# Moving the w2 product of an MLP block into the attention loop that precedes it, and its residual and statistics to other engines

## The chip, the core and the metric

The kernel runs on one core of a Trainium2 chip. The metric is the device time of one execution in microseconds (us). The unchanged kernel took 329.89 us (median of 3 runs, 329.3 to 330.42). "PE" is TensorE, whose matmuls write PSUM; "DVE" is VectorE; "ACT" is ScalarE; "POOL" is GpSimd, which here mostly issues DMAs. Each engine has an instruction stream of its own; for each wait the profile names the instruction or DMA that ended it, which it infers from semaphores.

## The reference

One sequence of S = 2048 tokens, width D = 512, bfloat16:

```python
xn = layernorm(x)
s  = A(xn)            # 32 heads of 16; each token attends to 8 tokens, 2 apart; then @ wo
g  = silu(B(xn))
out = x + s * g

def B(x):             # x is xn here
    h  = gelu(layernorm(x) @ w1)
    # each quarter of h's columns is shifted by one or two tokens, forwards or backwards
    hs = concat(shift(h, -1), shift(h, +1), shift(h, -2), shift(h, +2)) @ w2
    x1 = x + hs
    return x1 + gelu(layernorm(x1) @ w3) @ w4      # w3: 512 x 1376
```

Tokens lie in 16 tiles of 128. Attention goes in 4 passes of 4 tiles. Attention and the product with w2 both need results of earlier stages, but neither needs the other.

## The kernel before

The attention loop of one pass, cut. DVE forms the products of q with shifted k (`prodT`), PE sums them per head (`lgA`, `lgB`), ACT takes `exp`, PE transposes, DVE normalises, DVE forms the products with shifted v (`prodpv`), PE adds the eight of a tile into `po`, ACT copies it out, PE transposes it to `oT`.

```python
attv = paw.enter_context(tc.tile_pool(name="attv", bufs=2))
psL  = paw.enter_context(tc.tile_pool(name="psL", bufs=2, space=bass.MemoryType.PSUM))
for ps_ in range(NPASS):
    lgA = psL.tile([P, 512], dt.float32, name="lgA", tag="lg")
    lgB = psL.tile([P, 512], dt.float32, name="lgB", tag="lg")
    # ... 8 x prodT on DVE, 32 matmuls into lgA / lgB; exp on ACT; expR on PE; softmax on DVE ...
    for tb in range(4):
        t = 4 * ps_ + tb
        po = psA.tile([P, 512], dt.float32, name="po", tag="pA")
        vsh = attv.tile([P, W, D], dt.bfloat16, name="vsh")
        nc.gpsimd.dma_start(out=vsh[:], in_=src)              # 1 MB, 8 shifted copies of v
        for hf in range(2):
            prodpv = att4.tile([P, 4, D], dt.bfloat16, name="prodpv")
            nc.vector.tensor_tensor(out=prodpv[:]..., in0=vsh[:, 4*hf:4*hf+4, :]..., in1=Pn[...], op=ALU.mult)
            for wv in range(4):
                nc.tensor.matmul(po[:], lhsT=ident[:], rhs=prodpv[:, wv, :], ...)
        # ... ost (ACT), otp (PE), oT (ACT) ...
```

After the whole of attention comes the stage that the change takes apart, called "hs" below:

```python
for t in range(NT):
    pt = psB.tile([P, 512], dt.float32, name="pt_hs", tag="pT")
    for i in range(CH):                                            # CH = 4
        st0 = MGH + t * P + shifts[i]
        nc.tensor.matmul(pt[:], lhsT=hT[:, i, st0:st0 + P], rhs=w2s[:, i, :], start=(i == 0), stop=(i == CH - 1))
    nc.vector.tensor_tensor(out=x1[:, t, :], in0=pt[:], in1=xn[:, t, :], op=ALU.add)
    nc.vector.bn_stats(out=stats2[:, t, :], in_=x1[:, t, :])
    nc.vector.bn_aggr(out=mv2[:, t, :], in_=stats2[:, t, :])
nc.scalar.activation(out=rstd2[:], in_=mv2[:, :, 1:2], func=ACT.Sqrt, bias=eps_t[:], scale=1.0)
nc.vector.reciprocal(out=rstd2[:], in_=rstd2[:])
# ... then 4 units of: x2b = (x1 - mean) * rstd, transpose, @ w3, gelu, @ w4, epilogue ...
```

One `rstd2` serves all 16 tiles, so the first `x2b` cannot start before the last tile's statistics are there. The first start of `x2b` is therefore a good mark for the end of everything before the w3 stage.

The softmax here doesn't subtract the row's maximum and nothing guards it: scores larger than these inputs give would overflow.

## Time and profile before

| | before |
|---|---|
| profiled span | 328.5 us |
| busy: PE / DVE / ACT | 241.2 / 238.5 / 148.2 us |
| attention on DVE: first prodT to end of last prodpv | 99.8 to 197.1 us |
| hs stage and its lead-in, to the first x2b | 197.1 to 224.0 us |
| w3, gelu, w4 and epilogue, to the end | 104.5 us |

The page of the kernel before: the busy times, then the span in 40 slices of 8.2 us, each digit the busy share in tenths; PEclk is the clock granted to PE in tenths of full speed.

```profile
PE 241.2 (73%) x1216; PEld 105.8 (32%) x1216; DVE 238.5 (73%) x469; ACT 148.2 (45%) x240; POOL 57.9 (18%) x97
...
PE   0004899999943577588476587777799999999992
...
DVE  0879200002999999989997963995979979969964
...
PEclk9999999999995559959989659999999999999998
```

Slices 12 to 23 are attention: DVE is at 9 and PE between 3 and 8, with a clock that falls to half speed and comes back. Slices 24 to 27 are the hs stage. The averages of 73% for both engines hide this: each is the limit in another stage.

The groups of instructions, by line and shape: count, then busy us and mean ns of one, then idle time of the engine just before them and what ended it.

```profile
L280 PE MATMUL po<-prodpv,ident 128*128 128x512 bf16 x128 | 42.6, 485 | 7.2 <-DVE prodpv L273 7.0
L273 DVE TENSOR_TENSOR prodpv<-vsh,Pn 128x2048 bf16<-128x2048 bf16 x32 | 38.1, 1203 | 5.5 <-DMA vsh<-vscr 5.5
...
L310 PE MATMUL pt_hs<-w2s,hT 128*128 128x512 bf16 x64 | 15.2, 378 | 4.7 <-DVE x L311 4.0 <-ACT oT L287 0.7
L311 DVE TENSOR_TENSOR x<-pt_hs,xn 128x512 bf16<-128x512 f32 x16 | 10.5, 658 | 5.7 <-PE pt_hs L310 5.7
L312 DVE BATCH_NORM_STATS2 stats<-x 128x6 f32<-128x512 bf16 x16 | 10.3, 679 | 0.0
...
L313 DVE BATCH_NORM_AGGREGATE mv<-stats 128x2 f32<-128x6 f32 x16 | 2.7, 166 | 0.0
```

L311 to L313 are 23.5 us of DVE work. While it runs, PE has 15.2 us of matmuls to do and waits on DVE for 4.0 us; ACT has almost nothing. The 5.5 us before L273 are stalls in attention for the 1 MB loads of `vsh`, of which two buffers exist.

The timeline at the end of attention and around the hs stage (start, duration, engine, line, operation, tiles, count; in brackets the idle time before and what ended it).

```profile
193.41 3.54 PE L280 MATMUL po<-prodpv,ident 128*128 128x512 bf16 x8
194.70 2.36 DVE L273 TENSOR_TENSOR prodpv<-vsh,Pn 128x2048 bf16<-128x2048 bf16 x2 [1.20 <-DMA vsh<-vscr]
...
197.93 1.89 PE L280 MATMUL po<-prodpv,ident 128*128 128x512 bf16 x8
...
202.77 0.69 DVE L311 TENSOR_TENSOR x<-pt_hs,xn 128x512 bf16<-128x512 f32 x1 [5.71 <-PE pt_hs L310]
...
223.68 0.25 DVE L315 RECIPROCAL rstd<-rstd 128x16 f32<-128x16 f32 x1 [0.37 <-ACT rstd L314]
223.97 0.74 DVE L324 TENSOR_SCALAR x2b<-x,mv,rstd 128x512 bf16<-128x512 bf16 x2
```

DVE ends attention at 194.70 + 2.36 = 197.06 us, waits 5.71 us for the last two tiles to pass through PE and ACT, and then works 21 us without a break worth naming. Note the two `po` lines: the same eight matmuls take 3.54 us at one time and 1.89 us at another. That is the clock.

The windows view of the same run: length, busy time and count of each engine, granted clock, DMA share, GB/s.

```profile
100.00:113.00 13.00, 6.55 (x44) 1.86 (x43) 12.67 (x20) 3.11 (x4) 1.80 (x2) 0.50 0.45 163
113.00:136.00 23.00, 15.82 (x93) 5.96 (x93) 22.22 (x30) 5.88 (x10) 3.53 (x4) 0.81 0.50 181
...
181.00:198.00 17.00, 11.93 (x39) 4.20 (x37) 13.29 (x20) 2.98 (x5) 2.15 (x3) 0.60 0.42 149
```

Read across, the engines are PE, PE's weight loads, DVE, ACT and POOL. In the second row DVE is busy 22.22 of 23 us, and PE 15.82 at a mean clock of 0.81. The same view for the hs stage, one row:

```profile
201.00:224.00 23.00, 17.12 (x72) 6.90 (x71) 20.75 (x50) 2.19 (x3) 1.09 (x2) 1.00 0.28 100
```

Here the clock is 1.00 and DVE is busy 20.75 us from 202.77 on: a faster PE could shorten the wait ahead of this stage, but not these 21 us.

### The profile page before, as it was taken

Reading aid. Unit: us, or ns where it says so; the run is one execution under the profiler, and the core shown is the slowest. Engines: PE = TensorE matmul, PEld = TensorE weight load, DVE = VectorE, ACT = ScalarE, POOL = GpSimd, SP = SyncE. Lnnn points to the kernel's source line nnn. Section 1 sums busy time; section 2 is a strip of 40 time slices with the busy share of each in tenths; the row PEclk is TensorE's granted clock in tenths of the full one; section 3 lists DMA queues with packets and bytes.
Section 4 is the critical chain, followed back from the end, with each engine's and each line's share of the span. In section 5 each row is a group of like instructions: output and inputs, shape, how many; then the busy total and the mean of one; then the engine's idle time right before and its main releaser. Section 6 shows DMA issues by size and latency. Waiting matters only on the chain.

```text
span 328.5 us, 3542 instructions
## 1 busy us (share of the span) xinstructions
PE 241.2 (73%) x1216; PEld 105.8 (32%) x1216; DVE 238.5 (73%) x469; ACT 148.2 (45%) x240; POOL 57.9 (18%) x97
## 2 busy tenths in 40 slices
PE   0004899999943577588476587777799999999992
PEld 0003544444310222132122223333344444444440
DVE  0879200002999999989997963995979979969964
ACT  0023866667974022213223024005898479477320
POOL 4770000054002011122022103000000311211231
PEclk9999999999995559959989659999999999999998
DMA  7645440023001526546357358200000110210221
GB/s 252 218 145 122 96 66 0 0 113 130 16 0 45 213 89 233 189 151 236 126 190 254 129 196 301 75 2 1 0 2 0 64 65 2 75 52 18 80 80 48
DMA packets 19904, 33.46 MB, mean 102 GB/s; under 512 B 10176, under 2 KB 12240, under 8 KB 19888
## 3 DMA queue, kind: packets, MB, share of 16 engines
q0 software_dynamic: 8016, 26.60, 22.9%
q1 hardware_dynamic: 9760, 4.56, 6.1%
q10 hardware_dynamic: 2112, 2.10, 1.9%
q8 instruction: 9, 0.15, 0.2%
q14 instruction: 7, 0.06, 0.1%
HBM read 26.94 MB, written 4.21 MB: 95 GB/s over the span
## 4 chain that ended last, share of the span: by engine, by line
PE 34%; DVE 29%; DMA 12%; issue 10%; ACT 10%; POOL 3%; POOLq 0%; DVEq 0%; ACTq 0%
DMA vsh<-vscr 9%; PE pt_qk L163 8%; PE pt_w L335 8%; PE pt_w L360 5%; PE pt_v L175 4%; PE po L280 4%; DVE prodpv L273 4%; DVE stats L312 3%; DVE x L311 3%; DMA wvtmp<-in_A_wqkv_dram 3%; DVE prodT L223 2%; ACT yT L157 2%; ACT ub L350 2%; DVE xn L148 2%; DVE bout L365 2%
## 5 line engine op out<-in xcount | busy, mean ns | idle before, releaser
L280 PE MATMUL po<-prodpv,ident 128*128 128x512 bf16 x128 | 42.6, 485 | 7.2 <-DVE prodpv L273 7.0
L360 PE MATMUL pt_w<-w4s,zb 128*128 128x512 bf16 (+1 forms) x176 | 42.4, 379 | 0.0
L273 DVE TENSOR_TENSOR prodpv<-vsh,Pn 128x2048 bf16<-128x2048 bf16 x32 | 38.1, 1203 | 5.5 <-DMA vsh<-vscr 5.5
L335 PE MATMUL pt_w<-x2Tp,w3s 128*128 128x512 bf16 (+1 forms) x176 | 39.9, 379 | 2.3 <-ACT zb L340 2.0
L195 DVE TENSOR_TENSOR ub<-zb 128x512 bf16<-128x512 bf16 x16 | 6.6, 418 | 43.9 <-ACT zb L192 43.8
L223 DVE TENSOR_TENSOR prodT<-qT,kT 128x2048 bf16<-128x2048 bf16 x32 | 37.8, 1211 | 0.1
L270 POOL DMA_DIRECT2D vsh<-vscr x16 | 14.2, 886 | 90.1 <-DVE prodpv L273 68.3
L282 ACT ACTIVATE ost<-po 128x512 bf16<-128x512 f32 x16 | 9.6, 597 | 44.8 <-PE po L280 44.8
L155 PE MATMUL ytp<-ident,ybt 128*128 128x128 bf16 x64 | 6.8, 259 | 30.1 <-DVE ybt L152 29.4
L340 ACT ACTIVATE zb<-pt_w 128x512 bf16<-128x512 f32 (+1 forms) x44 | 25.3, 594 | 7.2 <-PE pt_w L335 7.0
L163 PE MATMUL pt_qk<-xnT,wqk 128*128 128x512 bf16 x128 | 27.8, 379 | 0.1
L377 POOL DMA_DIRECT2D out_dram<-ob x16 | 8.9, 558 | 105.5 <-DVE ob L376 105.5
L350 ACT ACTIVATE ub<-ub 128x1536 bf16<-128x1536 bf16 (+2 forms) x20 | 22.9, 1145 | 7.2 <-DVE ub L349 7.0
L335 PEld LDWEIGHTS <-w3s 128*128 128x128 bf16 (+1 forms) x176 | 17.6, 100 | 23.3 <-issue 4.3
L280 PEld LDWEIGHTS <-ident 128*128 128x128 bf16 x128 | 14.6, 117 | 27.6 <-issue 21.8
L360 PEld LDWEIGHTS <-zb 128*128 128x128 bf16 (+1 forms) x176 | 16.9, 98 | 19.3 <-DVE zb L351 0.4
L228 PE MATMUL lgA<-prodT,E 128*32 128x512 bf16 x64 | 8.3, 506 | 16.5 <-DVE prodT L223 16.4
L347 DVE TENSOR_TENSOR ub<-zb 128x1536 bf16<-128x1536 bf16 (+2 forms) x20 | 14.7, 739 | 7.3 <-ACT zb L340 7.1
L310 PE MATMUL pt_hs<-w2s,hT 128*128 128x512 bf16 x64 | 15.2, 378 | 4.7 <-DVE x L311 4.0
L178 POOL DMA_DIRECT2D vscr<-vst x16 | 8.7, 542 | 54.3 <-ACT vst L177 54.1
L163 PEld LDWEIGHTS <-wqk 128*128 128x128 bf16 x128 | 12.5, 98 | 15.1 <-issue 0.2
L367 ACT ACTIVATE sgo<-bout 128x512 bf16<-128x512 bf16 x16 | 10.0, 627 | 15.7 <-DVE bout L365 15.6
(86 smaller groups left out, 392.0 us busy)
## 6 DMA issues: line engine op xcount, KB each, us to landing
vsh<-vscr POOLq DMA_DIRECT2D x16, 1024.0 KB, 5.7
x_sb<-in_A_x_dram ACTq DMA_DIRECT2D x4, 512.0 KB, 10.2
vscr<-vst POOLq DMA_DIRECT2D x16, 128.0 KB, 2.0
xr<-in_A_x_dram POOLq DMA_DIRECT2D x16, 128.0 KB, 2.4
out_dram<-ob POOLq DMA_DIRECT2D x16, 128.0 KB, 2.0
w3s<-in_B_w_dram SPq DMA_DIRECT2D x1, 1376.0 KB, 7.0
w4s<-in_B_w_dram POOLq DMA_DIRECT2D x1, 1280.0 KB, 9.4
wqk<-in_A_wqkv_dram SPq DMA_DIRECT2D x1, 1024.0 KB, 7.6
```

The lines of the kernel that those rows point to most:

```text
L163: nc.tensor.matmul(pt[:], lhsT=wqk[:, c, 128 * j:128 * j + 128], rhs=xnT[:, 4 * ps_:4 * ps_ + 4, c, :], start=(c == 0), stop=(c == CH - 1),)
L175: nc.tensor.matmul(pt[:], lhsT=xnT[:, t, c, :], rhs=wvp[:, c, :], start=(c == 0), stop=(c == CH - 1))
L223: nc.vector.tensor_tensor(out=prodT[:], in0=qT[:, c, 512 * ps_:512 * ps_ + 512].unsqueeze(1).broadcast_to([P, 4, 512]), in1=kwin, op=ALU.mult,
L270: nc.gpsimd.dma_start(out=vsh[:], in_=src)
L273: nc.vector.tensor_tensor(out=prodpv[:].rearrange("p w (dh h) -> p w dh h", dh=DH), in0=vsh[:, 4 * hf:4 * hf + 4, :].rearrange("p w (dh h) ...
L280: nc.tensor.matmul(po[:], lhsT=ident[:], rhs=prodpv[:, wv, :], start=(hf == 0 and wv == 0), stop=(hf == 1 and wv == 3))
L310: nc.tensor.matmul(pt[:], lhsT=hT[:, i, st0:st0 + P], rhs=w2s[:, i, :], start=(i == 0), stop=(i == CH - 1))
L335: nc.tensor.matmul(pt[0:kj, :], lhsT=w3s[:, c, 128 * jj:128 * jj + kj], rhs=x2Tp[:, :, c, :], start=(c == 0), stop=(c == CH - 1),)
L340: nc.scalar.activation(out=zb[0:kj, jj, :], in_=pt[0:kj, :], func=ACT.Copy)
L347: nc.vector.tensor_tensor(out=ub[0:kj, j0:j1, :], in0=zb[0:kj, j0:j1, :], in1=zb[0:kj, j0:j1, :], op=ALU.mult)
L350: nc.scalar.activation(out=ub[0:kj, j0:j1, :], in_=ub[0:kj, j0:j1, :], func=ACT.Sigmoid, scale=GELU_K1)
L360: nc.tensor.matmul(pt[:], lhsT=h2p[0:kj, jj, tb * P:(tb + 1) * P], rhs=w4s[0:kj, jj, :], start=(jj == 0), stop=(jj == FCH - 1),)
```

## The change

Its intent is to take the hs stage off the critical path. The w2 matmuls go into the attention loop, where PE has room. The three DVE operations of a tile go away: the residual `xn` is added by four more matmuls into the same PSUM bank (transposed `xn` against slices of an identity), and the statistics come as accumulated sums of two ACT passes over that bank, a copy and a square. It also doubles the `vsh` buffers and loads w3 earlier. The core of the diff (the four units of the last stage are also renamed, with no effect on what they do):

```diff
+    identX = const.tile([P, CH, D], dt.bfloat16, name="identX")
+    nc.vector.memset(identX[:], 0.0)
+    for c in range(CH):
+        nc.vector.tensor_copy(out=identX[:, c, c * P:(c + 1) * P], in_=ident[:])
...
+            w3s = wts.tile([P, CH, F], dt.bfloat16, name="w3s")
+            # one element, so that the load cannot be issued before the last yT is there
+            nc.vector.tensor_copy(out=w3s[0:1, 0, 0:1], in_=yT[0:1, NT - 1, 0, 0:1])
+            nc.sync.dma_start(out=w3s[:], in_=B_w3.rearrange("(c p) n -> p c n", p=P))
...
-            attv = paw.enter_context(tc.tile_pool(name="attv", bufs=2))
+            attv = paw.enter_context(tc.tile_pool(name="attv", bufs=4))
... at the end of each attention pass:
+                for tb in range(4):
+                    t = 4 * ps_ + tb
+                    pths = psL.tile([P, 512], dt.float32, name="pt_hs", tag="lg")
+                    for i in range(CH):
+                        st0 = MGH + t * P + [-1, +1, -2, +2][i]
+                        nc.tensor.matmul(pths[:], lhsT=hT[:, i, st0:st0 + P], rhs=w2s[:, i, :], start=(i == 0), stop=False)
+                    for c in range(CH):
+                        nc.tensor.matmul(pths[:], lhsT=xnT[:, t, c, :], rhs=identX[:, c, :], start=False, stop=(c == CH - 1))
+                    nc.scalar.activation(out=x1[:, t, :], in_=pths[:], func=ACT.Copy, accum_out=sum2[:, t:t + 1])
+                    nc.scalar.activation(out=junk[:], in_=pths[:], func=ACT.Square, accum_out=sumsq2[:, t:t + 1])
... after the last pass:
+            # mean2 = sum2/D; rstd2 = 1/sqrt(sumsq2/D - mean2^2 + eps): four small DVE ops, Sqrt on ACT, reciprocal on DVE
... and the hs stage after attention is removed:
-            for t in range(NT):
-                pt = psB.tile([P, 512], dt.float32, name="pt_hs", tag="pT")
-                ...
-                nc.vector.tensor_tensor(out=x1[:, t, :], in0=pt[:], in1=xn[:, t, :], op=ALU.add)
-                nc.vector.bn_stats(out=stats2[:, t, :], in_=x1[:, t, :])
-                nc.vector.bn_aggr(out=mv2[:, t, :], in_=stats2[:, t, :])
```

More of the change, by code (lines that the diff above doesn't have):

```diff
@@ L111 @@
         hT = pre.tile([P, CH, MGH + S + MGH], dt.bfloat16, name="hT")
+        xnT = pre.tile([P, NT, CH, P], dt.bfloat16, name="xnT")
+        x1 = xn
+        sum2 = pre.tile([P, NT], dt.float32, name="sum2")
+        sumsq2 = pre.tile([P, NT], dt.float32, name="sumsq2")
+        mean2 = pre.tile([P, NT], dt.float32, name="mean2")
+        rstd2 = pre.tile([P, NT], dt.float32, name="rstd2")
+        junk = pre.tile([P, D], dt.bfloat16, name="junk", bufs=1)
         nc.vector.memset(hT[:, :, 0:MGH], 0.0)
@@ L122 @@
             xtp = tc.alloc_tile_pool(name="xtp", bufs=1)
-            xnT = xtp.tile([P, NT, CH, P], dt.bfloat16, name="xnT")
             yT = xtp.tile([P, NT, CH, P], dt.bfloat16, name="yT")
@@ L287 @@
                     nc.scalar.activation(out=oT[:, t, :, :], in_=otp[:], func=ACT.Copy)
+                for tb in range(4):
[8 more added lines that the diff above has]
+                    nc.scalar.activation(out=junk[:], in_=pths[:], func=ACT.Square, accum_out=sumsq2[:, t:t + 1])
+            shifts = [-1, +1, -2, +2]
+            nc.vector.tensor_scalar(out=mean2[:], in0=sum2[:], scalar1=1.0 / D, scalar2=None, op0=ALU.mult)
+            msq = pre.tile([P, NT], dt.float32, name="msq")
+            nc.vector.tensor_tensor(out=msq[:], in0=mean2[:], in1=mean2[:], op=ALU.mult)
+            nc.vector.tensor_scalar(out=rstd2[:], in0=sumsq2[:], scalar1=1.0 / D, scalar2=None, op0=ALU.mult)
+            nc.vector.tensor_tensor(out=rstd2[:], in0=rstd2[:], in1=msq[:], op=ALU.subtract)
+            nc.scalar.activation(out=rstd2[:], in_=rstd2[:], func=ACT.Sqrt, bias=eps_t[:], scale=1.0)
+            nc.vector.reciprocal(out=rstd2[:], in_=rstd2[:])
         with ExitStack() as phB:
@@ L293 @@
             psB = phB.enter_context(tc.tile_pool(name="psB", bufs=2, space=bass.MemoryType.PSUM))
-            w3s = b2k.tile([P, CH, F], dt.bfloat16, name="w3s")
-            nc.sync.dma_start(out=w3s[:], in_=B_w3.rearrange("(c p) n -> p c n", p=P))
             w4s = b2k.tile([P, FCH, D], dt.bfloat16, name="w4s")
@@ L299, with stage_x2_w3 @@
             nc.gpsimd.dma_start(out=w4s[0:FLAST, FCH - 1, :], in_=B_w4[(FCH - 1) * P:F, :])
-            shifts = [-1, +1, -2, +2]
-            x1 = b2k.tile([P, NT, D], dt.bfloat16, name="x1")
-            stats2 = b2k.tile([P, NT, 6], dt.float32, name="stats2")
-            mv2 = b2k.tile([P, NT, 2], dt.float32, name="mv2")
-            rstd2 = b2k.tile([P, NT, 1], dt.float32, name="rstd2")
-            for t in range(NT):
-                pt = psB.tile([P, 512], dt.float32, name="pt_hs", tag="pT")
-                for i in range(CH):
-                    st0 = MGH + t * P + shifts[i]
-                    nc.tensor.matmul(pt[:], lhsT=hT[:, i, st0:st0 + P], rhs=w2s[:, i, :], start=(i == 0), stop=(i == CH - 1))
-                nc.vector.tensor_tensor(out=x1[:, t, :], in0=pt[:], in1=xn[:, t, :], op=ALU.add)
-                nc.vector.bn_stats(out=stats2[:, t, :], in_=x1[:, t, :])
-                nc.vector.bn_aggr(out=mv2[:, t, :], in_=stats2[:, t, :])
-            nc.scalar.activation(out=rstd2[:], in_=mv2[:, :, 1:2], func=ACT.Sqrt, bias=eps_t[:], scale=1.0)
-            nc.vector.reciprocal(out=rstd2[:], in_=rstd2[:])
-            zbs = {}
-            def stage_x2_w3(ps_):
-                x2Tp = b2w.tile([P, 4, CH, P], dt.bfloat16, name="x2Tp")
-                for tb in range(4):
-                    t = 4 * ps_ + tb
+            zbs = {}
+            units = [list(range(4 * i, 4 * i + 4)) for i in range(NPASS)]
+            def stage_x2_w3(uq):
+                tiles = units[uq]
+                QT = P * len(tiles)
+                x2Tq = b2w.tile([P, 4, CH, P], dt.bfloat16, name="x2Tq")
+                for tb, t in enumerate(tiles):
                     x2b = b2w.tile([P, D], dt.bfloat16, name="x2b")
-                    nc.vector.tensor_scalar(out=x2b[:], in0=x1[:, t, :], scalar1=mv2[:, t, 0:1], scalar2=rstd2[:, t, :], op0=ALU.subtract, op1=ALU.mult)
+                    nc.vector.tensor_scalar(out=x2b[:], in0=x1[:, t, :], scalar1=mean2[:, t:t + 1], scalar2=rstd2[:, t:t + 1], op0=ALU.subtract, op1=ALU.mult)
                     x2ps = psB.tile([P, CH, P], dt.bfloat16, name="x2ps", tag="px2")
@@ L328, in stage_x2_w3 @@
                                          start=True, stop=True, is_transpose=True, skip_group_check=True)
-                    nc.scalar.activation(out=x2Tp[:, tb, :, :], in_=x2ps[:], func=ACT.Copy)
-                zb = b2b.tile([P, FCH, 512], dt.bfloat16, name="zb3")
+                    nc.scalar.activation(out=x2Tq[:, tb, :, :], in_=x2ps[:], func=ACT.Copy)
+                zb = b2b.tile([P, FCH, 4 * P], dt.bfloat16, name="zb3")
                 for jj in range(FCH):
                     kj = P if jj < FCH - 1 else FLAST
-                    pt = psB.tile([P, 512], dt.float32, name="pt_w3", tag="pW3")
+                    pt = psB.tile([P, 4 * P], dt.float32, name="pt_w3", tag="pW3")
@@ L334, in stage_x2_w3 @@
                     for c in range(CH):
                         nc.tensor.matmul(
-                            pt[0:kj, :], lhsT=w3s[:, c, 128 * jj:128 * jj + kj],
-                            rhs=x2Tp[:, :, c, :],
+                            pt[0:kj, 0:QT], lhsT=w3s[:, c, 128 * jj:128 * jj + kj],
+                            rhs=x2Tq[:, 0:len(tiles), c, :],
                             start=(c == 0), stop=(c == CH - 1),
                         )
-                    nc.scalar.activation(out=zb[0:kj, jj, :], in_=pt[0:kj, :], func=ACT.Copy)
@@ L341, in stage_x2_w3 @@
-                zbs[ps_] = zb
-            def stage_gelu_w4(ps_):
-                zb = zbs.pop(ps_)
-                ub = b2b.tile([P, FCH, 512], dt.bfloat16, name="ub3")
-                for (j0, j1, kj) in ((0, 3, P), (3, 6, P), (6, 8, P), (8, FCH - 1, P), (FCH - 1, FCH, FLAST)):
-                    nc.vector.tensor_tensor(out=ub[0:kj, j0:j1, :], in0=zb[0:kj, j0:j1, :], in1=zb[0:kj, j0:j1, :], op=ALU.mult)
-                    nc.vector.tensor_scalar(out=ub[0:kj, j0:j1, :], in0=ub[0:kj, j0:j1, :], scalar1=GELU_C3, scalar2=1.0, op0=ALU.mult, op1=ALU.add)
-                    nc.vector.tensor_tensor(out=ub[0:kj, j0:j1, :], in0=ub[0:kj, j0:j1, :], in1=zb[0:kj, j0:j1, :], op=ALU.mult)
-                    nc.scalar.activation(out=ub[0:kj, j0:j1, :], in_=ub[0:kj, j0:j1, :], func=ACT.Sigmoid, scale=GELU_K1)
-                    nc.vector.tensor_tensor(out=zb[0:kj, j0:j1, :], in0=zb[0:kj, j0:j1, :], in1=ub[0:kj, j0:j1, :], op=ALU.mult)
+                    nc.scalar.activation(out=zb[0:kj, jj, 0:QT], in_=pt[0:kj, 0:QT], func=ACT.Copy)
@@ new lines, in stage_x2_w3, with stage_gelu_w4 @@
+                zbs[uq] = zb
+            def stage_gelu_w4(uq):
+                tiles = units[uq]
+                QT = P * len(tiles)
+                zb = zbs.pop(uq)
+                ub = b2b.tile([P, FCH, 4 * P], dt.bfloat16, name="ub3")
+                for (j0, j1, kj) in ((0, 3, P), (3, 6, P), (6, 8, P), (8, FCH - 1, P), (FCH - 1, FCH, FLAST)):
+                    nc.vector.tensor_tensor(out=ub[0:kj, j0:j1, 0:QT], in0=zb[0:kj, j0:j1, 0:QT], in1=zb[0:kj, j0:j1, 0:QT], op=ALU.mult)
+                    nc.vector.tensor_scalar(out=ub[0:kj, j0:j1, 0:QT], in0=ub[0:kj, j0:j1, 0:QT], scalar1=GELU_C3, scalar2=1.0, op0=ALU.mult, op1=ALU.add)
+                    nc.vector.tensor_tensor(out=ub[0:kj, j0:j1, 0:QT], in0=ub[0:kj, j0:j1, 0:QT], in1=zb[0:kj, j0:j1, 0:QT], op=ALU.mult)
+                    nc.scalar.activation(out=ub[0:kj, j0:j1, 0:QT], in_=ub[0:kj, j0:j1, 0:QT], func=ACT.Sigmoid, scale=GELU_K1)
+                    nc.vector.tensor_tensor(out=zb[0:kj, j0:j1, 0:QT], in0=zb[0:kj, j0:j1, 0:QT], in1=ub[0:kj, j0:j1, 0:QT], op=ALU.mult)
@@ L352, in stage_gelu_w4 @@
                 h2p = zb
-                for tb in range(4):
-                    t = 4 * ps_ + tb
+                for tb, t in enumerate(tiles):
                     xr = b2w.tile([P, D], dt.bfloat16, name="xr")
@@ L377, in stage_gelu_w4 @@
                     nc.gpsimd.dma_start(out=out2d[t * P:(t + 1) * P, :], in_=ob[:])
-            for q in range(NPASS + 1):
-                if q < NPASS:
-                    stage_x2_w3(q)
-                if q >= 1:
-                    stage_gelu_w4(q - 1)
+            for uq in range(len(units) + 1):
+                if uq < len(units):
+                    stage_x2_w3(uq)
+                if uq >= 1:
+                    stage_gelu_w4(uq - 1)
 _INS = ['A_x', 'A_wqkv', 'A_wo', 'B_x', 'B_w1', 'B_w2', 'B_w3', 'B_w4']
```

## The prediction

> **What bounds it now.** By the timeline and the chain of waits, the 328.5 us span has stages. Attention (100 to 202 us) is bound by VectorE (DVE): 32 products prodT (1.21 us each), 32 prodpv (1.20 us), 16 softmax groups. DVE idles there about 7 us: 5.5 us for vsh loads (groups by line), 1.8 us for expR. TensorE (PE) is half idle; the windows view gives a granted clock of 0.50 to 0.92. Then a serial "hs" stage, from 201.7 us to the first x2b at 224.0: 22 us in which DVE does 16 x (add 0.66, bn_stats 0.68, bn_aggr 0.17 us) while PE's 64 matmuls and ScalarE (ACT, 1.2 us busy) mostly wait. The last 104 us (w3/gelu/w4) are full on PE and DVE.
>
> **What the change does.**
> - Removes those 48 DVE instructions (10.5 + 10.3 + 2.7 us busy). The residual becomes 64 more PE matmuls (identX), the statistics two ACT passes per tile with accumulated sums (32 x about 0.6 us, estimated from the 597 ns PSUM copies).
> - Moves hs into the attention loop. The instruction order shows its matmuls between lgB, expR and po, its ACT work between exp and ost.
> - Four vsh buffers instead of two; w3 loads during the q/k stage.
> - Adds on DVE: a memset and four copies in the prologue (0.5 us of it on the statistics there), some 1 us at the head of attention (prodT is no longer interleaved with the last gelu pieces), four tiny ops at its end.
>
> **Does it fit?** Per pass of 4 tiles DVE needs 22.3 us. PE gets 32 more matmuls: 6.9 us at 216 ns; by the timeline's durations it then needs 3.2 (lg) + 0.6 (expR) + 7 (po) + 1.6 (otp) + 6.9 = 19.3 us. That fits at full clock, not at half (8 po matmuls take 1.89 us at full clock, 3.57 at half). The Trainium skill, "TensorE: Matmul & The Clock Gate", Part 1, says that the throttled state is the default and activity releases it; the two po durations agree. So denser PE work should raise the clock and shorten the tail (the last po groups take 3.6 us now). ACT goes from 6 to about 11 us of a pass. I expect 2 to 4 us of new DVE stalls, mostly in pass 0, where PE starts cold, against 7 us of vsh and expR waits removed.
>
> **Sum.** DVE's attention work ends near 194 us (102.3 start + 88.5 + 0.5 + 3 of stalls) against 197.1. The square root sits on ACT behind the last ost/oT pairs, so x2b starts 2.5 us later, at 196.7 instead of 224.0. The rest is unchanged; w4 has landed in time. 329.9 - 27 = 303 us; range 298 to 310.
> Chances: faster by over 2% 0.97, within 2% 0.02, slower 0.01.
>
> **What would show it.** DVE's wait for vsh near 0; x2b begins at 195 to 199 us; from there to the end still 104 us; granted clock over 0.9 in attention after pass 0; PE busy up by 25 us, ACT up by 18, DVE down by 23.
>
> **What would make it wrong.** PE staying at half clock in attention, so that hs delays po and DVE stalls on full prodpv buffers (5 us a pass); ACT's in-order queue delaying exp behind hs evacuations, or an accumulating ACTIVATE costing much more than 0.6 us; the two PSUM buffers shared by lg and hs serialising passes; rstd2 or w4 arriving late.

## The result and the profile after

The changed kernel took 304.72 us (median of 12 runs, 303.89 to 306.84) against 329.6 us (15 runs, 327.86 to 332.77) of the kernel before in the same rounds. The ratio is 0.9248, 95% interval 0.9219 to 0.9277. Ratios here are the mean time of one kernel's fast runs over that of the other's of the same rounds, so they are not quite the ratio of the medians quoted. Both profiles are of fast runs, with spans of 328.5 and 302.1 us. The results are correct, as are those of every experiment below.

| | before | predicted | after |
|---|---|---|---|
| time, median | 329.6 us | 303.0 us | 304.72 us |
| DVE ends attention | 197.06 us | 194 us | 194.82 us |
| first x2b | 223.97 us | 196.7 us | 196.78 us |
| first x2b to end | 104.5 us | 104 us | 105.3 us |

The page of the changed kernel, the same lines:

```profile
PE 240.0 (79%) x1280; PEld 108.6 (36%) x1280; DVE 219.8 (73%) x431; ACT 167.5 (55%) x304; POOL 57.9 (19%) x97
...
PE   0000999999994279889889889788999999999991
...
DVE  1698600000399998999999979839799899789873
...
PEclk9999999999999569999999999999999999999997
```

From the second slice of attention on, PE digits between 3 and 8 have become 7 to 9, and the clock stays up after its first dip. DVE lost 18.7 us of work and the span lost 26.4.

The groups after:

```profile
L287 DVE TENSOR_TENSOR prodpv<-vsh,Pn 128x2048 bf16<-128x2048 bf16 x32 | 37.8, 1193 | 0.0
...
L294 PE MATMUL po<-prodpv,ident 128*128 128x512 bf16 x128 | 32.7, 379 | 0.6 <-DVE prodpv L287 0.2
L307 PE MATMUL pt_hs<-w2s,hT 128*128 128x512 bf16 x64 | 19.1, 395 | 3.7 <-ACT junk L311 2.9 <-ACT expT L249 0.8
L309 PE MATMUL pt_hs<-identX,xnT 128*128 128x512 bf16 x64 | 17.8, 380 | 0.0
...
L310 ACT ACTIVATE xn<-pt_hs 128x512 bf16<-128x512 f32 x16 | 9.6, 597 | 24.1 <-PE pt_hs L309 24.1
...
L311 ACT ACTIVATE junk<-pt_hs 128x512 bf16<-128x512 f32 x16 | 9.4, 590 | 0.0
...
L311 ACT ACTIVATION_READ_ACCUMULATOR junk<-pt_hs 128x1 f32 x16 | 3.2, 203 | 0.0
L310 ACT ACTIVATION_READ_ACCUMULATOR xn<-pt_hs 128x1 f32 x16 | 3.1, 194 | 0.0
```

The wait for `vsh` is 0.0. The `po` matmuls average 379 ns instead of 485. Each accumulating activation brings a second instruction that reads the accumulator, 0.19 to 0.20 us.

DVE's waits from 95 to 200 us, after (total, times, longest); before, this stretch had 5.5 us for `vsh` and 1.8 us for `expR`:

```profile
DVE den L265 <- PE expR L258: 3.9, 4, 2.7
DVE x2b L341 <- PE x2ps L344: 1.4, 2, 1.0
DVE rstd L320 <- ACT rstd L319: 1.4, 1, 1.4
DVE hT L213 <- ACT ub L212: 0.4, 1, 0.4
```

The timeline at the end of attention, after:

```profile
192.46 2.36 DVE L287 TENSOR_TENSOR prodpv<-vsh,Pn 128x2048 bf16<-128x2048 bf16 x2
...
194.04 1.89 PE L294 MATMUL po<-prodpv,ident 128*128 128x512 bf16 x8
194.24 0.60 ACT L301 ACTIVATE oT<-otp 128x512 bf16<-128x512 bf16 x1 [0.49 <-PE otp L299]
...
194.86 1.28 ACT L319 ACT_TABLE_LOAD   x1
...
196.15 0.31 ACT L319 ACTIVATE rstd<-rstd,eps_t 128x16 f32<-128x16 f32 x1
...
196.49 0.25 DVE L320 RECIPROCAL rstd<-rstd 128x16 f32<-128x16 f32 x1 [1.38 <-ACT rstd L319]
196.78 0.74 DVE L341 TENSOR_SCALAR x2b<-xn,mean,rstd 128x512 bf16<-128x512 bf16 x2
```

From the end of DVE's attention work to the first `x2b` it is now 196.78 - 194.82 = 1.96 us, where it was 223.97 - 197.06 = 26.91 us. That is 24.95 of the 27.19 us by which `x2b` starts earlier; the other 2.24 us come from attention itself ending earlier. The last stage gave back 0.8 us.

The windows of attention, after:

```profile
100.00:113.00 13.00, 7.27 (x41) 1.75 (x42) 12.36 (x17) 3.25 (x5) 3.54 (x4) 0.57 0.71 233
113.00:136.00 23.00, 19.71 (x122) 8.31 (x121) 22.23 (x33) 11.67 (x31) 3.53 (x4) 1.00 0.69 235
...
181.00:198.00 17.00, 13.76 (x78) 6.25 (x77) 14.30 (x27) 9.91 (x22) 1.09 (x2) 1.00 0.33 99
```

In the second row DVE does as much as before (22.23 us), while PE gets 122 matmuls done instead of 93 and ACT 11.67 us of work instead of 5.88. The clock is 1.00 from there on. The Trainium skill, "TensorE: Matmul & The Clock Gate", Part 1, says that PE is throttled by default and that activity releases it; these traces agree, with a clock of 1.00 in the second row where it was 0.81 with fewer matmuls, and eight `po` matmuls at 1.89 us against 3.54 us. Experiment 6 shows that more matmuls did not raise the clock in every stretch.

### The profile page after: what moved, and what is told of

Same layout as the page of the kernel before. It is cut to its first block, busy times and chain, and to the rows that moved or that the text cites. A ratio compares the mean times of both kernels' runs of the same rounds, so it can differ in the third digit from the quotient of the medians.

```text
span 302.1 us, 3695 instructions
## 1 busy us (share of the span) xinstructions
PE 240.0 (79%) x1280; PEld 108.6 (36%) x1280; DVE 219.8 (73%) x431; ACT 167.5 (55%) x304; POOL 57.9 (19%) x97
## 3 DMA queue, kind: packets, MB, share of 16 engines
q0 software_dynamic: 8016, 26.60, 26.4%
## 5 line engine op out<-in xcount | busy, mean ns | idle before, releaser
L352 PE MATMUL pt_w<-x2Tq,w3s 128*128 128x512 bf16 (+1 forms) x176 | 39.9, 379 | 1.5 <-ACT zb L357 1.4
L294 PE MATMUL po<-prodpv,ident 128*128 128x512 bf16 x128 | 32.7, 379 | 0.6 <-DVE prodpv L287 0.2
L378 PEld LDWEIGHTS <-zb 128*128 128x128 bf16 (+1 forms) x176 | 16.9, 98 | 19.3 <-DVE zb L370 0.4
L310 ACT ACTIVATE xn<-pt_hs 128x512 bf16<-128x512 f32 x16 | 9.6, 597 | 24.1 <-PE pt_hs L309 24.1
L307 PE MATMUL pt_hs<-w2s,hT 128*128 128x512 bf16 x64 | 19.1, 395 | 3.7 <-ACT junk L311 2.9
L309 PE MATMUL pt_hs<-identX,xnT 128*128 128x512 bf16 x64 | 17.8, 380 | 0.0
```

Source lines behind the costliest of these rows:

```text
L307: nc.tensor.matmul(pths[:], lhsT=hT[:, i, st0:st0 + P], rhs=w2s[:, i, :], start=(i == 0), stop=False)
L309: nc.tensor.matmul(pths[:], lhsT=xnT[:, t, c, :], rhs=identX[:, c, :], start=False, stop=(c == CH - 1))
L352: nc.tensor.matmul(pt[0:kj, 0:QT], lhsT=w3s[:, c, 128 * jj:128 * jj + kj], rhs=x2Tq[:, 0:len(tiles), c, :], start=(c == 0), stop=(c == CH ...
L378: nc.tensor.matmul(pt[:], lhsT=h2p[0:kj, jj, tb * P:(tb + 1) * P], rhs=w4s[0:kj, jj, :], start=(jj == 0), stop=(jj == FCH - 1),)
```

## The experiments

The theory: DVE bounds attention, and its 21 us in the hs stage were serial time. The gain needs both halves of the change: the work has to leave DVE, and what replaces it has to lie under attention. The rivals: either half alone gives most of it; the extra `vsh` buffers, or the early w3, or the warmer PE clock do. The last three experiments look for what is still to be had.

### 1. The change with two vsh buffers

```diff
-            attv = paw.enter_context(tc.tile_pool(name="attv", bufs=4))
+            attv = paw.enter_context(tc.tile_pool(name="attv", bufs=2))
```

> The changed kernel with two vsh buffers instead of four. Theory A (the gain is the hs stage leaving DVE and the critical path; the vsh buffers are a small extra): DVE's waits for vsh come back, some 3 to 5 us, so 307 to 310 us. Theory B (the deeper prefetch carries much of the gain): 315 us or more. If the buffers do nothing: 304 to 305 us.

Measured: 309.7 us (309.21 to 309.99), ratio to before 0.9395 (0.9368 to 0.9421). DVE's waits of this run have the old line back:

```profile
DVE prodpv L287 <- DMA vsh<-vscr: 4.3, 6, 1.3
```

The first `x2b` comes at 200.70 us. So the buffers are worth 5.0 us of the change's 24.9 (medians of different rounds), and the rest does without them.

### 2. The kernel before with four vsh buffers

```diff
-            attv = paw.enter_context(tc.tile_pool(name="attv", bufs=2))
+            attv = paw.enter_context(tc.tile_pool(name="attv", bufs=4))
```

> The kernel before with four vsh buffers and nothing else. Theory A: of the 5.5 us of vsh waits the 3.0 us of the first three passes are saved, the 2.5 us of the last pass are hidden behind the slow po groups of PE: about 326 to 327 us. Theory B: 315 us or less.

Measured: 325.85 us (324.24 to 331.25, the last a slow run), ratio 0.987 (0.9829 to 0.991). The fast runs have a median of 325.65 us. The wait for `vsh` is gone. The buffers alone give about 3.7 us here, close to the expected 326 to 327 us.

### 3. The move alone

The w2 matmuls are in the attention loop, but the add and the statistics stay on DVE, right behind them. Cut: the tiles for the statistics, the stop flag of the w2 matmuls and the code behind the loop change to fit.

```diff
-                    for c in range(CH):
-                        nc.tensor.matmul(pths[:], lhsT=xnT[:, t, c, :], rhs=identX[:, c, :], start=False, stop=(c == CH - 1))
-                    nc.scalar.activation(out=x1[:, t, :], in_=pths[:], func=ACT.Copy, accum_out=sum2[:, t:t + 1])
-                    nc.scalar.activation(out=junk[:], in_=pths[:], func=ACT.Square, accum_out=sumsq2[:, t:t + 1])
+                    nc.vector.tensor_tensor(out=x1[:, t, :], in0=pths[:], in1=xn[:, t, :], op=ALU.add)
+                    nc.vector.bn_stats(out=stats2[:, t, :], in_=x1[:, t, :])
+                    nc.vector.bn_aggr(out=mv2[:, t, :], in_=stats2[:, t, :])
```

> The changed kernel, but with the DVE add, bn_stats and bn_aggr kept inside the attention loop (no identity matmuls, no ACT statistics). Theory A (attention is DVE-bound, so DVE work moved into it costs its full length): DVE gets 16 x 1.27 = 20 us more in attention, x2b starts near 215 us, total 320 to 324 us. Theory C (the serial hs stage was lost to waiting between engines, and the overlap alone pays): 303 to 309 us.

Measured: 322.03 us (320.78 to 322.4), ratio 0.9763 (0.9731 to 0.9796), as expected. DVE is busy 239.2 us, as in the kernel before, and the first `x2b` comes at 216.17 us. Moving work of the engine that bounds the loop into that loop only makes the loop longer. What the move can save is DVE's wait for the first w2 product behind attention, 5.4 us in experiment 2; by the medians of fast runs it saved 3.6 us. (The comparison is not quite clean: the versions built on the change come to attention's first `prodpv` about 1 us later, here at 118.0 us, in the kernel before at 116.6.)

### 4. The offload alone

The identity matmuls and the ACT statistics are there, but as a stage after attention, in the place of the old one.

```diff
+            for t in range(NT):      # after attention, not in its passes
+                pths = psB.tile([P, 512], dt.float32, name="pt_hs", tag="pT")
+                ... 4 matmuls with w2s, 4 with identX, Copy and Square with accum_out ...
```

> The changed kernel with the hs stage put back after attention, where it stood, but with residual on PE and statistics on ACT. Theory A (only both together pay): ACT becomes the limit of a still serial stage, about 16 x 1.2 us = 19 us, so total 322 to 326 us (the vsh buffers' 3 us included). Theory D (taking the work off DVE is what pays): 310 us or less.

Measured: 337.97 us (336.17 to 342.83); the fast runs are 336.17, 336.57 and 339.37, ratio 1.0235 (1.0178 to 1.0293). The expectation of 322 to 326 us was missed: this is slower than the kernel before, though whether by more than 2% is unclear. I had ACT as the limit of the new serial stage; the trace shows PE. The timeline of ACT's copies of four successive tiles (the profile fell in the run of 342.83 us, slow, but in this stage the matmuls have their full rate):

```profile
206.31 0.60 ACT L321 ACTIVATE xn<-pt_hs 128x512 bf16<-128x512 f32 x1 [2.02 <-PE pt_hs L320]
...
207.99 0.60 ACT L321 ACTIVATE xn<-pt_hs 128x512 bf16<-128x512 f32 x1 [0.41 <-PE pt_hs L320]
...
209.72 0.60 ACT L321 ACTIVATE xn<-pt_hs 128x512 bf16<-128x512 f32 x1 [0.46 <-PE pt_hs L320]
...
211.44 0.60 ACT L321 ACTIVATE xn<-pt_hs 128x512 bf16<-128x512 f32 x1 [0.46 <-PE pt_hs L320]
```

Tiles follow each other at 1.72 to 1.73 us, which is 8 matmuls of 216 ns, and ACT waits for PE each time. From the first w2 matmul (204.34) to the first `x2b` (235.37) it is 31 us, where the old stage took 22.3 (201.65 to 223.97). These 8.7 us are most of the 10.9 us by which the fast runs (median 336.57) are behind those of experiment 2; the first `prodpv`, at 117.8 us here and at 116.6 in the kernel before, is about 1 us more. The same eight matmuls and two activations that cost little under attention are worse than the DVE work they replace when nothing covers them.

### 5. The change with w3 loaded late

```diff
-            w3s = wts.tile([P, CH, F], dt.bfloat16, name="w3s")
-            nc.vector.tensor_copy(out=w3s[0:1, 0, 0:1], in_=yT[0:1, NT - 1, 0, 0:1])
-            nc.sync.dma_start(out=w3s[:], in_=B_w3.rearrange("(c p) n -> p c n", p=P))
... in the last phase:
+            w3s = b2k.tile([P, CH, F], dt.bfloat16, name="w3s")
+            nc.sync.dma_start(out=w3s[:], in_=B_w3.rearrange("(c p) n -> p c n", p=P))
```

> The changed kernel with the w3 load put back to the start of the last phase. If the early load matters, the first w3 matmul waits for a 1.4 MB load of some 7 us: 308 to 312 us. Theory A (it is only a safeguard, since the load can still be issued when the last prodT is done, some 20 us ahead of its first use): 304 to 306 us.

Measured: 304.82 us (303.9 to 305.13), ratio 0.9254: no difference. The early load is not what the change lives on.

### 6. The kernel before with a busier PE

Eight useless matmuls ahead of each tile's `po` sums; they are overwritten, so the result stays right.

```diff
+                    for i in range(8):
+                        nc.tensor.matmul(po[:], lhsT=ident[:], rhs=w2s[:, i % CH, :], start=True, stop=True)
```

> The kernel before with 128 useless matmuls (8 into each po buffer, overwritten by the real group) so that PE is as busy in attention as in the changed kernel and its clock stays up. Theory A: only the cold tail of attention shrinks, since DVE sets the pace elsewhere: 326 to 328 us. Theory E (the slow PE clock in attention was a main cost and the extra matmuls repaired it): 320 us or less.

Measured: 331.49 us (327.87 to 333.42), ratio 1.0032 (0.9948 to 1.0115): the same. The expectation was missed. The profile (of a slow run) has a clock of 1.00 from 181 to 202 us, where the kernel before has 0.67, and DVE waits 4.0 us instead of 5.7 for the first w2 product. But its waits for `expR` grew from 1.8 to 4.9 us, probably because the added matmuls stand ahead of `expR` on PE, which was not tested. The clock of the whole run rose only from 0.919 to 0.943, and from 113 to 136 us it was lower, 0.71 against 0.81, so this is a weak test of the clock. What it does say is that these added matmuls gained nothing. That the clock alone does not explain 25 us is shown better by the hs stage of the kernel before, with 20.75 us of DVE work at a clock of 1.00.

### 7. The change with ACT's tables loaded early

In the timeline after, a table load of 1.28 us stands in the chain to `x2b`. This run puts one-element activations where ACT is free, so that each later switch of function finds its table loaded.

```diff
+    tbl = const.tile([P, 4], dt.float32, name="tbl")
... behind the loads of x:
+                    nc.scalar.activation(out=tbl[:, 0:1], in_=eps_t[:], func=ACT.Sqrt)
... behind the last square root of the prologue:
+                        if t == 1:
+                            nc.scalar.activation(out=tbl[:, 1:2], in_=xn[:, t, 0:1], func=ACT.Sigmoid)
... behind exp:
+                if ps_ == NPASS - 1:
+                    nc.scalar.activation(out=tbl[:, 2:3], in_=expT[:, 1, 0:1], func=ACT.Sqrt)
... behind the first unit's x2Tq:
+                if uq == 0:
+                    nc.scalar.activation(out=tbl[:, 3:4], in_=x2Tq[:, 3, 0, 0:1], func=ACT.Sigmoid)
```

> An attempt to beat the changed kernel: four one-element activations make ACT load its sqrt and sigmoid tables where it idles, not on the chain (four loads of 1.28 us: before the first rstd, before the first gelu, before rstd2, before the first w3 gelu). If those loads are on the chain as the trace says, 3 to 4.5 us less than the changed kernel: 300 to 302 us. If they are hidden: 304 to 305 us.

Measured: 301.55 us (301.27 to 302.06), ratio 0.9164 (0.9116 to 0.9213). Experiment 5, equal to the change, ran in the same rounds at 304.82 (ratio 0.9254). This is the fastest version. Its timeline at the end of attention:

```profile
190.71 2.36 DVE L293 TENSOR_TENSOR prodpv<-vsh,Pn 128x2048 bf16<-128x2048 bf16 x2
...
193.40 0.31 ACT L325 ACTIVATE rstd<-rstd,eps_t 128x16 f32<-128x16 f32 x1 [0.31 <-DVE rstd L324]
...
193.73 0.25 DVE L326 RECIPROCAL rstd<-rstd 128x16 f32<-128x16 f32 x1 [0.37 <-ACT rstd L325]
194.02 0.83 DVE L347 TENSOR_SCALAR x2b<-xn,mean,rstd 128x512 bf16<-128x512 bf16 x2
```

From the start of the last `prodpv` pair to `x2b` it is 3.31 us instead of 4.32: 1.0 us at this square root. The other 1.75 us by which `x2b` is earlier come from before attention, where DVE's first gelu operation starts at 78.52 instead of 80.14 us (ahead of gelu's own table load, so most of it is not that load's). The fourth preload shows no gain: from `x2b` to the end it is 105.5 us, 105.3 in the change.

The Trainium skill, "ScalarE: Activation LUTs", section "Table sets: the hidden batching unit", says that tables come in named sets and that `exp` and `sqrt` belong to different ones; the loads in these traces stand just at the changes of function, as that says.

### 8. The change with the residual added on DVE

The identity matmuls go; DVE adds `xn` inside the loop, and ACT takes the two sums from the result (cut: both activations now read `x1`, and the w2 matmuls carry the stop flag).

```diff
-                    for c in range(CH):
-                        nc.tensor.matmul(pths[:], lhsT=xnT[:, t, c, :], rhs=identX[:, c, :], start=False, stop=(c == CH - 1))
+                    nc.vector.tensor_tensor(out=x1[:, t, :], in0=pths[:], in1=xn[:, t, :], op=ALU.add)
```

> The changed kernel with the residual added by DVE in the loop (16 adds of 0.66 us, 0.57 us apart when back to back) instead of by 64 identity matmuls; the statistics stay on ACT, reading x1. Theory A (every us of DVE work in attention is a us of time): 304.7 + 9 = 312 to 315 us. If PE or ACT sets the pace instead: 304 us or less.

Measured: 310.72 us (310.1 to 311.99), ratio 0.9442 (0.9396 to 0.9489). That is 6.0 us worse than the change (5.9 against experiment 5 of the same rounds), less than the expected 312 to 315 us. DVE's busy time rises by 9.3 us to 229.1, but its waits for `expR` fall from 3.9 to 1.4 us, with 64 matmuls fewer on PE. Doing an addition with 64 matmuls looks wasteful, and it pays because PE has room in this loop and DVE has none.

### 9. The w2 tiles in the first three passes only

Five, five and six tiles in passes 0 to 2, none in the last, so that the chain to `rstd2` is finished before attention ends.

```diff
-                for tb in range(4):
-                    t = 4 * ps_ + tb
+                for t in [range(0, 5), range(5, 10), range(10, 16), range(0)][ps_]:
```

> The changed kernel with the 16 hs tiles spread over the first three passes (5, 5, 6) instead of 4 in each, so that rstd2 is ready before the last pass ends and no hs work stands in front of its expR. Theory A with PE slack: DVE's 2.7 us wait for expR in the last pass and the 2.1 us of the rstd2 chain shrink, 301 to 303 us. Theory F (hs also keeps PE's clock up in the last pass, and PE has no room for a fifth tile per pass): po runs at half clock again in the last pass and DVE stalls in the others, 305 us or more.

Measured: 308.97 us (308.33 to 309.22), ratio 0.9357 (0.9273 to 0.944): 4 us slower than the change. The window of the last pass, then the timeline behind it:

```profile
181.00:198.00 17.00, 10.07 (x50) 3.93 (x50) 14.95 (x28) 4.67 (x8) 1.48 (x2) 0.70 0.28 83
```

```profile
199.21 0.73 DVE L340 TENSOR_SCALAR x2b<-xn,mean,rstd 128x512 bf16<-128x512 bf16 x2
...
202.94 0.74 DVE L340 TENSOR_SCALAR x2b<-xn,mean,rstd 128x512 bf16<-128x512 bf16 x2 [3.00 <-PE x2ps L343]
```

The square root is indeed out of the way: `x2b` follows the last `prodpv` at once. But that last `prodpv` pair itself starts at 196.81 instead of 192.46 us. The fuller passes make DVE wait on PE at places where it did not (`lgA`, 3.3 us). And without the w2 matmuls the last pass falls back to a clock of 0.70, where the change has 1.00, so the third `x2b` waits 3.00 us for PE to get through its backlog, where it waited 0.99.

### 10. Experiments 7 and 9 together

> The same spread on top of the version with early table loads (301.6 us). Theory A: 298.5 to 300 us, less than the sum of both, since the sqrt load is off the chain already. Theory F: 302 us or more.

Measured: 308.97 us (305.7 to 309.57), ratio 0.9334 (0.9249 to 0.9419). The clock of the last window is 0.74, and DVE waits 5.1 us for `x2ps` in all. Spreading over three passes also loses with the tables loaded early, 7.4 us by the medians (of different rounds). The profile is of the run of 305.70 us; the three others took 308.89 to 309.57.

## Why the prediction was right, and where it was not

**The main step held.** The prediction said that the 22 us of the hs stage, from 201.7 us to the first `x2b`, would go, since the other engines have room under attention. The first `x2b` was predicted for 196.7 us and came at 196.78. Experiments 2, 3, 4 and the change make a square, all with four `vsh` buffers, in medians of fast runs. (3, 4 and the change also load w3 early, neutral in experiment 5, and reach the first `prodpv` at 117.4 to 118.0 us, the kernel before at 116.6, so the steps away from 2 look about 1 us worse than the moves alone are.)

| | statistics on DVE | on PE and ACT |
|---|---|---|
| hs after attention | 325.65 us | 336.57 us |
| hs in the attention loop | 322.03 us | 304.72 us |

Moving alone gives 3.6 us, offloading alone loses 10.9, both give 20.9. The parts do not add up, because each half changes what the other runs into: DVE-bound work moved under a DVE-bound loop lengthens it, and offloaded work that nothing covers is bounded by PE at 1.73 us a tile, where DVE needed about 1.26 (in the kernel before, its adds of two tiles start at 207.30 and, two tiles later, at 209.81).

**The vsh buffers held.** 5.5 us of waits were there to be removed; experiments 1 and 2 measure 5.0 and 3.7 us.

**New stalls, right in size, wrong in place.** The prediction had 2 to 4 us of new DVE stalls, mostly in pass 0. There are 3.9 us of waits for `expR`, where the prediction had counted the 1.8 us of the kernel before as removed; only 0.47 us of them is in pass 0, and the longest, 2.65 us, is in the last pass. The end of attention was put at "near 194"; it came at 194.82.

**The chain to rstd2: shorter than predicted, and another one.** The prediction put the square root behind the last `ost` and `oT`, 2.5 us after attention. The trace has 1.96 us, of which 1.28 are a table load that the prediction does not name; the last `ost` starts at 196.37, behind the square root. Attention ended 0.8 us late and this chain was 0.5 us short, so the match of `x2b` to 0.1 us is partly luck.

**The accumulating activations.** The estimate of 0.6 us a pass did not know of the separate accumulator read of 0.19 to 0.20 us. Much of it overlaps: in the middle passes a copy and a square together take 1.26 us from start to end. ACT rose by 19.3 us against 18 predicted.

**PE busy up by 25 us: wrong.** It went from 241.2 to 240.0. The prediction does not say how it got 25. New are only the 64 identity matmuls: 13.8 us at 216 ns, or 24.3 us if each is taken at the 380 ns of its record, which overlaps the next. And the other matmuls of attention took less, since the clock rose: the `po` group alone fell from 42.6 to 32.7 us. The Trainium skill, "Perfetto Trace Analysis", section "Identifying the Most-Contended Engine", says that matmul busy time is not a good measure of how close a kernel is to roofline, because pipelined instructions look smaller in the trace; here 64 more matmuls left it at 240 us, but the clock changed too, so no run here shows that reason apart.

**DVE busy down by 23 us: too much.** It fell by 18.7. The prediction added up the three groups (23.5 us), but neighbouring instructions overlap in the record: in the window from 201 to 224 us, DVE's busy time is 20.75 us in all. The setup of the identity and the small operations took about 2 us back. This did not touch the predicted time, which was read from the timeline.

**The size of the whole.** By the two profiled runs the gain was 26.4 us, against 27 predicted. The medians say 24.9, since the profiled run of the kernel before took 330.24 us, 0.6 above its median, and that of the change 303.89, 0.8 below.

**The clock.** Predicted over 0.9 after pass 0, measured 1.00. It is not the main source of the gain: the hs stage kept DVE busy 20.75 us at a clock of 1.00, and the clock could only touch the 5.71 us of waiting ahead of it (4.0 in experiment 6, with a clock of 1.00 there). How much of attention's own 2.24 us the clock gave was not separated; experiment 6 is too weak for that. Experiment 9 shows that losing it in the last pass goes along with a delay, but it moved work between passes at the same time, so how many of its 4 us the clock cost stays open. Open too is why the last stage takes 0.8 us longer than before; its waits for `x2ps` are 2.3 us against 1.4.

## What to carry to other kernels

Before moving a stage under a loop, ask which engine bounds the loop, and take that engine's share out of the stage first; before offloading a stage, ask what will cover it, since neither half need pay alone. An addition done by spare matmuls can be worth it where DVE is the limit, as 64 matmuls were worth 6 us here. When a stage is gone, read the new chain for small things that it used to hide: one-element activations that load ACT's tables early gave another 3.3 us, 1.0 us of it at the square root that the old stage had hidden.

## What the Trainium skill lacked or had wrong

- "ScalarE: Activation LUTs", section "What ACT_TABLE_LOAD costs", puts a switch of table set at 1283 ns for the load and about 1380 ns for a drain, some 2.66 us in all. The load agrees (1.28 us). The drain does not show here: at the end of attention ACT's last copy ends at 194.24 + 0.60 = 194.84 us, the load starts at 194.86, and the square root starts at 196.15, so the switch costs 1.31 us. Taking it off the chain gained 1.0 us.
- The same page says that an activation can give an accumulator output, but neither it nor another page gives the price on ScalarE. Here each one adds an ACTIVATION_READ_ACCUMULATOR of 0.19 to 0.20 us, 32 of them; a copy and a square of 128x512 with both reads took 1.26 us.
